# Layer 1's first matrix is applied to a batch's 256 state rows, and the softmax weights multiply the result

## The chip, the cores and the metric

The kernel runs on one core of a Trainium2 chip. The metric is the device time of one execution in microseconds. The names of the engines are those of the profile: PE (TensorE) does matmuls, PEld loads their weights, DVE (VectorE), ACT (ScalarE) and POOL (GpSimd) work on elements, and SP's queue issues the transfers.

## The reference

Three steps follow each other: attention between 512 tokens and 32 states for each of 8 batches and 8 heads (head size 64), a layer normalisation with a two-matrix block and a residual, and a gated convolution block. The 544 tokens of a batch are the 512 token reads and the 32 state reads. All weights are float64.

```python
scores = scale * np.matmul(x, state.transpose(0, 1, 3, 2))
...
xread = np.matmul(a, state)                  # a: softmax over the 32 states
...
sread = np.matmul(a2, x)                     # a2: softmax over the 512 tokens
return np.concatenate([xread, sread], axis=2).astype(np.float32)
...
mu = np.mean(x, axis=-1, keepdims=True)
var = np.mean((x - mu) ** 2, axis=-1, keepdims=True)
xn = (x - mu) / np.sqrt(var + 1e-06) * g_ln
ch = np.maximum(xn @ w_ch1, 0.0) @ w_ch2     # 512 -> 2048 -> 512
return (x + ch).astype(np.float32)
...
h = np.maximum(x @ w_in, 0.0)                # 512 -> 1024
...
return (h * gate @ w_out).astype(np.float32) # gate: sigmoid of a 3-tap convolution of h
```

## The kernel before

Everything is held transposed: features on the 128 partitions, tokens along the free axis. A product in nearly full precision is three matmuls of numbers that are split into a high and a low part (`three`, lines L565 to L567). The float64 words of a weight are taken apart, joined and split by a chain that runs over ACT (L184, L185), DVE (L190, L191), POOL (L192), ACT (L219) and POOL (L220), one slice of 512 KB at a time (class `Converter`).

Layer 1 runs in units: batches 0 to 6, then the tail unit (the 256 state reads of all batches together, `NB`, 256 columns), then batch 7 (`LAST`). In a unit, `L1(u, m)` makes 128 of the 2048 hidden values for all tokens in the bank `ph`, contracting 512 features in four chunks; ACT (L583) and DVE (L584) make the two parts `hH` and `hL` of its relu; and `L2(u, m, n)` adds its contribution to the four banks `acc`. The loop over m from 0 to 15 calls `L1(u, m + 1)` and `L2(u, m)`. Between them it advances a generator, `tasks`, with the attention and the layer normalisation of the next batch, which use the two banks `pat`. At the end of a unit `residual` adds `acc` to the batch's tokens `XT` (L595) and stores them to DRAM (L597). Layer 2 follows after all units.

Attention makes scores twice: tokens by states, and states by tokens (`scores`, L254, in plain fp32, two matmuls that each fill 64 of the bank's 128 partitions). The softmax weights of the tokens, transposed (32 states of four heads fill the 128 partitions), multiply the states to give the token reads: `token_read`, L335 and L336, two matmuls of 512 columns for each 128 features, eight per batch. `lnorm` takes mean and variance by matmuls with a matrix of ones (L487, L488), subtracts the mean (L500), and multiplies by one over the deviation (L510); `xn_split` multiplies by `gcol` and splits into `xnH` and `xnL` (L523, L524), on which L1 works.

Batch 0 has a path of its own through the start (`tokens_start`, in two halves of 256 columns), and while units 0's products run, the weights of layer 1 are still being converted: `need` waits for the slice, and `order` lists in which order the slices are converted. The order of the instructions on each engine is set by the tile scheduler from the program's order, its priorities and its own model of the times.

Of the kernel before, what the change touches and what calls it, by code (L numbers as in the profile page):

```python
# [42 lines left out]
def kernel(  # L43
# [29 lines left out]
    xnH = new("xnH", [KC, S], F32R)  # L73
    xnL = new("xnL", [KC, S], F32R)
# [5 lines left out]
    s_bd = new("s_bd", [KC, 64])  # L80
    s_raw = new("s_raw", [KC, P])
    s_H = new("s_H", [KC, P], F32R)
    s_L = new("s_L", [KC, P], F32R)
    ident = new("ident", [P])
# [10 lines left out]
    spare = [f"w{a}_{m}" for m in range(LATE, M1) for a in (1, 2)]  # L95

    WARM = 8
    START = "s00ws0abab01cac0001b10w1a0cb010a011bL1wcaLbLwc1wLc11L1LwLLLLLL"

    EARLY = 6  # L100
# [15 lines left out]


# [11 lines left out]
    def load_raw(b, s):  # L129
        for hh in range(2):  # L130
            r = 64 * s + 32 * hh
            nc.sync.dma_start(
                s_raw[r : r + 32, :, 64 * hh : 64 * hh + 64],
                state[b].rearrange("(q hh) n d -> hh n q d", hh=2)[hh],
            )
# [33 lines left out]

    def load_rows(tag, w, m):  # L170
# [23 lines left out]
    class Converter:  # L194


        def __init__(self, total, temps, sub):
            self.total, self.temps, self.sub = total, temps, sub
# [14 lines left out]
        def third(self):  # L213
            if self.n2 < self.n1:
                i = self.n2
                (tag, _), t = self.raw[i], self.tmp[i]
                self.done[i] = new(tag, [2, DM], F32R)
# [16 lines left out]
    def prep_state():  # L234
        V.transpose(s_bd.rearrange("p q m -> p (q m)"), s_in.rearrange("p q h r -> p (q h r)"))
        state_parts()

    def state_parts(sub=V):
        A.activation(s_H, s_raw, AF.Copy)
        for ql in range(2):  # L240
            r = slice(64 * ql, 64 * ql + 64)

            def part(t):
                return t[r].rearrange("p (g ql) m -> p ql g m", g=2)[:, ql]

            sub.tensor_tensor(part(s_L), part(s_raw), f32(part(s_H)), op=ALU.subtract)
# [4 lines left out]
    def scores(b, g, xT):  # L251
        sc = bank()
        for ql in range(2):
            T.matmul(  # L254
                sc[64 * ql : 64 * ql + 64, :], s_bd[:, 2 * g + ql, :], xT[:, ql, :],
# [727 lines left out]
```

## Time and profile before

| | us |
|---|---|
| median of 3 runs | 1287.51 (1287.22 to 1288.11) |
| the profiled execution | 1287.5 |
| its span, first to last instruction | 1285.7 |
| busy: PE / DVE / ACT / POOL | 1245.7 / 692.1 / 459.5 / 283.6 |

The span is what the profile's rows add up to; the execution's time is 1.8 us longer. A busy PE is one that had a matmul in flight: its rows overlap, so the cost of one is read from start to start, its pitch, and not from its duration. An "x4" or "x2" in a row of PE counts instructions: an fp32 matmul is two of them.

### The profile page before, as it was taken

The page shows a single profiled execution, that of the slowest core. Times are in us where ns is not written, and L with a number is a line of the kernel's source. Part 1 is how long each engine was busy: PE and PEld are TensorE (multiplying, and loading weights), DVE is VectorE, ACT ScalarE, POOL GpSimd, SP SyncE. Part 2 cuts the span into 40 slices and gives each one's busy share as a digit, 9 for nine tenths or more (in the row PEclk, how much of TensorE's full clock was granted, in tenths as well). Part 3 has the DMA queues.
Part 4 walks back from the last instruction along what each step waited for, and adds up shares of the span by engine and source line. Part 5 has one row for each costly group of instructions (what it writes and reads, how often), then busy time and mean ns, then how long its engine had stood idle before and what let it go on. Part 6 is the DMA issues. An engine that isn't in the chain of part 4 may idle for free.

```text
span 1285.7 us, 15045 instructions
## 1 busy us (share of the span) xinstructions
PE 1245.7 (97%) x5827; PEld 1000.4 (78%) x5827; DVE 692.1 (54%) x1050; ACT 459.5 (36%) x807; POOL 283.6 (22%) x381
## 2 busy tenths in 40 slices
PE   6888899999999999999999999999999999999997
PEld 5665677877787877877877889888888888888885
DVE  5999974444444443444444332544555665566653
ACT  5855432222232222222222222445343343344332
POOL 3477701101101100200200210343233222122210
PEclk9899999999999999999999999999999999999999
DMA  9641022012012002012003000333110111110001
GB/s 310 182 115 52 5 66 39 17 47 42 17 49 40 17 34 52 20 35 48 17 1 82 1 23 28 108 91 107 57 49 23 61 66 32 42 67 1 33 33 41
DMA packets 126148, 69.10 MB, mean 54 GB/s; under 512 B 103268, under 2 KB 115580, under 8 KB 125052
## 3 DMA queue, kind: packets, MB, share of 16 engines
q1 hardware_dynamic: 126076, 68.14, 18.9%
q8 instruction: 45, 0.74, 0.2%
q14 instruction: 27, 0.22, 0.1%
HBM read 50.82 MB, written 17.30 MB: 53 GB/s over the span
## 4 chain that ended last, share of the span: by engine, by line
PE 87%; DVE 7%; DMA 1%; SPq 1%; issue 1%; POOL 1%; ACT 1%; DVEq 0%; POOLq 0%
PE acc L565 14%; PE acc L566 14%; PE acc L567 13%; PE ph L567 12%; PE ph L565 12%; PE ph L566 12%; PE pat L565 2%; PE pat L566 2%; PE pat L567 2%; DVE ctmp L191 2%; PE pat L254 1%; PE pat L281 1%; DVE ctmp L190 1%; DMA w<-in_moe_w_ch_dram 1%; PE pat L335 1%
## 5 line engine op out<-in xcount | busy, mean ns | idle before, releaser
L565 PE MATMUL ph<-xnH,w 128*128 128x512 f32 (+1 forms) x684 | 258.1, 377 | 2.9 <-DVE w L584 1.4
L566 PE MATMUL ph<-xnL,w 128*128 128x512 f32 (+1 forms) x684 | 257.8, 377 | 1.4 <-POOL xnL L467 1.4
L567 PE MATMUL ph<-xnH,w 128*128 128x512 f32 (+1 forms) x684 | 257.5, 376 | 0.2 <-POOL w L220 0.2
L566 PE MATMUL acc<-hL,w 128*128 128x512 f32 (+1 forms) x560 | 213.6, 385 | 6.4 <-DVE hL L584 6.4
L567 PE MATMUL acc<-hH,w 128*128 128x512 f32 (+1 forms) x560 | 212.1, 382 | 0.0
L584 DVE SCALAR_TENSOR_TENSOR hL<-ph,hH 128x512 fp32r<-128x512 f32 (+1 forms) x142 | 92.4, 651 | 198.8 <-ACT hH L583 198.2
L565 PE MATMUL acc<-hH,w 128*128 128x512 f32 (+1 forms) x560 | 188.2, 383 | 0.1
L583 ACT ACTIVATE hH<-ph 128x512 fp32r<-128x512 f32 (+1 forms) x142 | 80.3, 566 | 278.8 <-PE ph L567 267.1
L565 PEld LDWEIGHTS ph<-xnH,w 128*128 128x128 f32 x684 | 128.7, 188 | 34.1 <-issue 5.0
L567 PEld LDWEIGHTS ph<-xnH,w 128*128 128x128 f32 x684 | 129.0, 189 | 30.2 <-issue 5.7
L566 PEld LDWEIGHTS ph<-xnL,w 128*128 128x128 f32 x684 | 128.8, 188 | 27.2 <-POOL xnL L467 1.9
L566 PEld LDWEIGHTS acc<-hL,w 128*128 128x128 f32 x560 | 105.6, 189 | 31.4 <-DVE hL L584 10.5
L900 DVE SCALAR_TENSOR_TENSOR w<-w,cw,w 128x544 f32<-128x544 f32 x128 | 105.3, 823 | 45.8 <-POOL w L898 44.0
L567 PEld LDWEIGHTS acc<-hH,w 128*128 128x128 f32 x560 | 105.7, 189 | 22.1 <-issue 1.0
L565 PEld LDWEIGHTS acc<-hH,w 128*128 128x128 f32 x560 | 101.7, 189 | 22.4 <-issue 0.7
L566 PE MATMUL acc<-w,w 128*128 128x512 f32 x272 | 107.8, 396 | 0.0
L565 PE MATMUL acc<-w,w 128*128 128x512 f32 x272 | 107.3, 395 | 0.0
L567 PE MATMUL acc<-w,w 128*128 128x512 f32 x272 | 105.7, 396 | 0.0
L479 POOL TENSOR_TENSOR bR<-XT 128x512 f32<-128x512 f32 x12 | 16.5, 1376 | 378.3 <-ACT XT L369 377.8
L881 ACT ACTIVATE w<-w 128x544 f32<-128x544 f32 x64 | 42.2, 659 | 150.8 <-DVE w L900 150.7
L882 DVE TENSOR_TENSOR w<-w,w 128x544 f32<-128x544 f32 x64 | 46.7, 729 | 51.9 <-ACT w L881 51.9
L888 DVE TENSOR_TENSOR w<-w,w 128x512 fp32r<-128x512 f32 x64 | 46.8, 731 | 42.6 <-ACT w L887 40.4
(284 smaller groups left out, 1790.6 us busy)
## 6 DMA issues: line engine op xcount, KB each, us to landing
w<-in_moe_w_ch_dram SPq DMA_DIRECT2D x32, 512.0 KB, 6.8
out_dram<-w SPq DMA_DIRECT2D x34, 256.0 KB, 2.2
x2d<-XT SPq DMA_DIRECT2D x8, 1024.0 KB, 3.9
bP<-in_x_dram SPq DMA_DIRECT2D x104, 64.0 KB, 2.5
bP<-in_x_dram SPq DMA_DIRECT2D x24, 256.0 KB, 3.3
bP<-x2d SPq DMA_DIRECT2D x8, 512.0 KB, 3.8
bQ<-x2d SPq DMA_DIRECT2D x8, 512.0 KB, 4.4
w<-in_moe_w_in_dram SPq DMA_DIRECT2D x8, 512.0 KB, 3.7
```

The costliest lines, as they stand in the source:

```text
L190: V.tensor_scalar(t, t, 3, None, op0=ALU.logical_shift_left)
L191: V.scalar_tensor_tensor(t, hi, -(2**31), t, op0=ALU.bitwise_and, op1=ALU.bitwise_or)
L479: add.tensor_tensor(sp, src[:, 0:2], src[:, 2:4], op=ALU.add)
L565: T.matmul(o, lh, rh, start=first, stop=False)
L566: T.matmul(o, lh, rl, start=False, stop=False)
L567: T.matmul(o, ll, rh, start=False, stop=last)
L583: A.activation(h, p, AF.Relu)
L584: V.scalar_tensor_tensor(l, p, 0.0, f32(h), op0=ALU.max, op1=ALU.subtract)
L881: A.activation(c, c, AF.Sigmoid)
L882: V.tensor_tensor(c, c, h[:, 1 : SEQ + 1], op=ALU.mult)
L888: V.tensor_tensor(g[:, 1], c[:, :S], f32(g[:, 0]), op=ALU.subtract)
L900: V.scalar_tensor_tensor(c, h[:, k : k + SEQ], cw[:, k * FF + f : k * FF + f + 1], c, op0=ALU.mult, op1=ALU.add,)
```

## The change

The token reads are a product of the softmax weights A (256 rows: 8 heads x 32 states) with the states, laid out block by block. So L1 of the tokens is the same as A times Z, where Z is (states less their mean) times (g times W1): 256 rows by 2048. L1 then contracts 256 rows and not 512 features, and has six matmuls where it had twelve (L597 to L599). One over the deviation of the layer normalisation is positive and one number per token, so it passes through the relu and the second matrix, and `residual` multiplies by it (L648) before it adds (L650).

Added is the making of Z. Each batch has eight tiles (`z_tile`: 4 column blocks `j` of 512 by 2 halves `g` of the states), each with two fp32 matmuls of 64 partitions (L562) into a bank `pat`, one DVE instruction that subtracts the mean (L569), and the split into `ZH` on ACT (L572) and `ZL` on DVE (L573), through one buffer `zc`. A second `Z` pair lets block j + 1 be made while block j is used. The first matrix is converted in unit 0 only, times g, in rows and unsplit, written to DRAM (`w1d`), and from unit 1 on streamed back in pieces of 512 KB through a ring of seven buffers (`pass_pairs`, L556), eight pieces per batch.

`token_read` contracts only the 64 rows that a group of 128 features needs, and has three matmuls for it where it had two: twelve per batch (L361). L510 and the splits of the normalised tokens (L523, L524) are gone. For the tail unit L1 is a product in plain fp32 (L625), of the streamed pieces and the normalised state reads. Batch 0 no longer makes its normalised tokens in the start; Z of block j is made when four slices of the first matrix are converted (`z_first`), and slices are converted four of the first, four of the second matrix a time.

```diff
-    def token_weights_3(aT, Y):
-
-        A.activation(Y[0:64, 0], aT[0:64], AF.Copy)
-        A.activation(Y[64:128, 1], aT[64:128], AF.Copy)
-        V.tensor_tensor(Y[64:128, 0], aT[0:64], f32(Y[0:64, 0]), op=ALU.subtract)
-        V.tensor_tensor(Y[0:64, 1], aT[64:128], f32(Y[64:128, 1]), op=ALU.subtract)
-
-    def token_read(xr, q, Y):
-        T.matmul(xr, s_H[:, q], Y, start=True, stop=False)
-        T.matmul(xr, s_L[:, q], Y, start=False, stop=True)
...
+    def token_weights_3(aT, b, g, c):
+        h, l = (t[:, g, c] for t in parts[b])
+        A.activation(h, aT, AF.Copy)
+        V.tensor_tensor(l, aT, f32(h), op=ALU.subtract)
+
+    def token_read(b, g):
+
+        h, l = (t[:, g] for t in parts[b])
+        xr = [bank(), bank()]
+        for i, (s, a) in enumerate(((s_H, h), (s_L, h), (s_H, l))):
+            for ql in range(2):
+                r = slice(64 * ql, 64 * ql + 64)
+                T.matmul(xr[ql], s[r, 2 * g + ql], a[r], start=i == 0, stop=i == 2)
+        for ql in range(2):
+            A.activation(XT[b][:, 2 * g + ql], xr[ql], AF.Copy)
...
+    def pass_pairs(n):
+
+        for _ in range(n):
+            i = passed[0]
+            if i == len(stream):
+                return
+            passed[0] += 1
+            _, j, g = stream[i]
+            t = pieces[stream[i]] = new(f"r{i % RING}", [2, S])
+            nc.sync.dma_start(flat(t), w1d[j, g])
+
+    def z_tile(u, j, g, w):
+
+        zp = bank()
+        for ql in range(2):
+            T.matmul(
+                zp[64 * ql : 64 * ql + 64], sbd[u][:, 2 * g + ql], w[:, ql], start=True, stop=True
+            )
+        if g == 0:
+            Z[u, j] = [new(f"Z{c}{j % 2}", [2, S], F32R) for c in "HL"]
+        h, l = (t[:, g] for t in Z[u, j])
+        f = new("zc", [S])
+        V.scalar_tensor_tensor(
+            f, colsum[j // 2][:, j % 2], nbars[u][:, g : g + 1], zp, op0=ALU.mult, op1=ALU.add
+        )
+        A.activation(h, f, AF.Copy)
+        V.tensor_tensor(l, f, f32(h), op=ALU.subtract)
+
+    def z_step(u, j, g):
+        z_tile(u, j, g, pieces[u, j, g])
+        pass_pairs(1)
+
+    def z_first(j):
+
+        for q in range(KC):
+            need(1, KC * j + q)
+        w = rounded[2 * j : 2 * j + 2]
+        sums = new("zc", [S])
+        G.tensor_tensor(sums, w[0][:, 0], w[0][:, 1], op=ALU.add)
+        for q in range(2):
+            G.tensor_tensor(sums, sums, w[1][:, q], op=ALU.add)
+        vp = bank()
+        T.matmul(vp, ones1, sums, start=True, stop=True)
+        A.activation(colsum[j // 2][:, j % 2], vp, AF.Copy)
+        for g in range(2):
+            z_tile(0, j, g, w[g])
+            nc.sync.dma_start(w1d[j, g], flat(w[g]))
...
-        cols_product(p, w1[m], *([t[:, k, c] for k in range(KC)] for t in (xnH, xnL)))
...
+    def L1(u, m):
+        c = slice(P * (m % 4), P * (m % 4) + P)
+        if u < NB:
+            p = ph[m % 2]
+            (wh, wl), (ah, al) = Z[u, m // 4], parts[u]
+            for g in range(2):
+                three(p, wh[:, g, c], wl[:, g, c], ah[:, g], al[:, g], g == 0, g == 1)
+        else:
+            p = ph[m % 2][:, :TAIL]
+            for k in range(KC):
+                w = pieces["t", m // 4, k // 2][:, k % 2]
+                T.matmul(p, w[:, c], tns[NB][:, k], start=k == 0, stop=k == KC - 1)
+            if m % 4 == 3:
+                pass_pairs(2)
+        relu_parts(m, p)
...
-            V.tensor_tensor(dst[:, d, :n], dst[:, d, :n], acc[d][:, :n], op=ALU.add)
...
+        for d in range(KC):
+            V.tensor_tensor(t[d], acc[d], rstd[u], op=ALU.mult)
+        for d in range(KC):
+            V.tensor_tensor(XT[u][:, d], XT[u][:, d], t[d], op=ALU.add)
+        nc.sync.dma_start(x2d[u], flat(XT[u]))
...
+            if u == 0 and m % 4 == 2 and m < 12:
+                z_first(m // 4 + 1)
+            elif m % 4 < 2 and 0 < u < NB and m < 12:
+                z_step(u, m // 4 + 1, m % 4)
+            elif m in (12, 13) and ahead is not None:
+                z_step(ahead, 0, m - 12)
```

The order of the instructions moves in three places that matter below. First PE, in unit 1, at `L1(1, 13)`. Before, its twelve matmuls stand together, four such groups of three (two of them here):

```order
L565 MATMUL ph1_84<-xnH_1_63,w1_13_157_1192 128x512
L566 MATMUL ph1_84<-xnL_2_64,w1_13_157_1192 128x512
L567 MATMUL ph1_84<-xnH_1_63,w1_13_157_1192 128x512
L565 MATMUL ph1_84<-xnH_1_63,w1_13_157_1192 128x512
L566 MATMUL ph1_84<-xnL_2_64,w1_13_157_1192 128x512
L567 MATMUL ph1_84<-xnH_1_63,w1_13_157_1192 128x512
```

After the change, the last tile of block 3 (`r0`, `sbd1`: batch 1) and the first of the next batch (`r1`, `sbd0`) stand at this place, both in the bank `pat1`, then the second halves of `L1` for m = 12 and 13 with the matmuls of the layer normalisation (L467, L468) in between:

```order
L599 MATMUL ph1_83<-AH1_107_647,ZL1_251_1703 128x512
L562 MATMUL pat1_85<-r0_199_1240,sbd1_109_649 64x512 x2
L562 MATMUL pat1_85<-r1_201_1268,sbd0_206_1331 64x512 x2
L597 MATMUL ph0_82<-AH1_107_647,ZH1_250_1702 128x512
L598 MATMUL ph0_82<-AL1_108_648,ZH1_250_1702 128x512
L597 MATMUL ph1_83<-AH1_107_647,ZH1_250_1702 128x512
L598 MATMUL ph1_83<-AL1_108_648,ZH1_250_1702 128x512
L467 MATMUL pat0_84<-bQ_260_1750,ones_11_73 128x512
L599 MATMUL ph0_82<-AH1_107_647,ZL1_251_1703 128x512
L599 MATMUL ph1_83<-AH1_107_647,ZL1_251_1703 128x512
L468 MATMUL pat0_84<-bQ_260_1750,ones_11_73 128x512
L562 MATMUL pat1_85<-r3_215_1393,sbd0_206_1331 64x512 x2
```

What moved: an L1 is in two halves of three matmuls here, and the second half stands right behind the tile of Z that it reads.

Second PE, in unit 1, at the token read of batch 2. Before, two matmuls for each bank:

```order
L566 MATMUL ph0_83<-xnL_2_64,w1_2_58_334 128x512
L567 MATMUL ph0_83<-xnH_1_63,w1_2_58_334 128x512
L335 MATMUL pat0_85<-bQ_185_1601,s_H_9_71 128x512
L336 MATMUL pat0_85<-bQ_185_1601,s_L_10_72 128x512
L565 MATMUL acc0_79<-hH_3_65,w2_1_95_728 128x512
L335 MATMUL pat1_86<-bQ_185_1601,s_H_9_71 128x512
L336 MATMUL pat1_86<-bQ_185_1601,s_L_10_72 128x512
```

After, three for each, and those of the second bank stand twenty rows further on:

```order
L298 MATMUL pat1_85<-bP_213_1362,bV_221_1419 64x128 x8
L361 MATMUL pat0_84<-AH0_204_1329,s_H_6_68 128x512
L361 MATMUL pat0_84<-AH0_204_1329,s_L_7_69 128x512
L361 MATMUL pat0_84<-AL0_205_1330,s_H_6_68 128x512
L597 MATMUL acc0_78<-hH_1_63,w2_3_68_417 128x512
L598 MATMUL acc0_78<-hL_2_64,w2_3_68_417 128x512
L599 MATMUL acc0_78<-hH_1_63,w2_3_68_417 128x512
```

The rows of one bank stand together, so matmuls of the two row halves do not alternate here (they do in some other batches).

Third DVE, at the end of unit 1. Before, four additions from the banks `acc`, and then the relu of the next unit:

```order
L595 TENSOR_TENSOR XT1_91_706<-XT1_91_706,acc0_79 128x512
L324 TENSOR_TENSOR bU_218_2155<-bU_218_2155,m10_219_2156 128x512
L595 TENSOR_TENSOR XT1_91_706<-XT1_91_706,acc1_80 128x512
L595 TENSOR_TENSOR XT1_91_706<-XT1_91_706,acc2_81 128x512
L325 STREAM_TRANSPOSE bR_221_2181<-bU_218_2155 128x512
L595 TENSOR_TENSOR XT1_91_706<-XT1_91_706,acc3_82 128x512
L584 SCALAR_TENSOR_TENSOR hL_4_66<-ph0_83,hH_3_65 128x512
L331 TENSOR_TENSOR bQ_223_2216<-bR_221_2181,bQ_223_2216 64x512
```

After, four multiplications from the banks, and the relu parts (L612) of the next unit between the additions:

```order
L648 TENSOR_TENSOR tn_267_1891<-acc0_78,rs1_165_1058 128x512
L648 TENSOR_TENSOR tn_267_1891<-acc1_79,rs1_165_1058 128x512
L333 TENSOR_REDUCE m10_285_1991<-bU_284_1990 128x16
L310 RECIPROCAL z20_283_1986<-z20_283_1986 128x1
L648 TENSOR_TENSOR tn_267_1891<-acc2_80,rs1_165_1058 128x512
L648 TENSOR_TENSOR tn_267_1891<-acc3_81,rs1_165_1058 128x512
L650 TENSOR_TENSOR XT1_106_646<-XT1_106_646,tn_267_1891 128x512 x2
L612 SCALAR_TENSOR_TENSOR hL_2_64<-ph0_82,hH_1_63 128x512
L334 TENSOR_TENSOR bU_284_1990<-bU_284_1990,m10_285_1991 128x512
L311 TENSOR_SCALAR rm0_289_2047<-hmask_14_76,z20_283_1986 128x2
L650 TENSOR_TENSOR XT1_106_646<-XT1_106_646,tn_267_1891 128x512
L612 SCALAR_TENSOR_TENSOR hL_2_64<-ph1_83,hH_1_63 128x512
```

The relu of the next unit's first L1 now has six instructions of the residual ahead of it, where it had four.

## Rows read from the trace of the kernel before

**Rows 1.** The page: the span, and the busy time of the engines.

```profile
span 1285.7 us, 15045 instructions
...
PE 1245.7 (97%) x5827; PEld 1000.4 (78%) x5827; DVE 692.1 (54%) x1050; ACT 459.5 (36%) x807; POOL 283.6 (22%) x381
```

**Rows 2.** Windows: length, then each engine's busy time, granted clock, DMA share, GB/s.

```profile
80.00:100.00 20.00, 18.08 (x86) 13.78 (x85) 19.77 (x25) 11.52 (x21) 15.23 (x11) 0.91 0.22 65
140.00:160.00 20.00, 17.21 (x70) 12.42 (x69) 19.03 (x23) 8.54 (x13) 13.70 (x10) 1.00 0.02 4
160.00:180.00 20.00, 20.00 (x82) 14.48 (x82) 15.32 (x26) 7.69 (x13) 0.00 (x0) 1.00 0.12 26
267.80:366.00 98.20, 98.20 (x445) 76.20 (x445) 47.48 (x85) 27.26 (x46) 8.45 (x8) 1.00 0.15 35
814.00:901.00 87.00, 87.00 (x383) 70.98 (x382) 40.94 (x66) 41.31 (x71) 34.65 (x32) 1.00 0.38 116
```

**Rows 3.** Timeline of PE, steady stretch: start, us, line, operation, tiles.

```profile
300.50 0.39 PE L565 MATMUL ph<-xnH,w 128*128 128x512 f32 x1
300.73 0.39 PE L566 MATMUL ph<-xnL,w 128*128 128x512 f32 x1
```

**Rows 4.** Timeline of PE in the tail unit, matmuls of 256 columns.

```profile
769.01 0.28 PE L566 MATMUL ph<-xnL,w 128*128 128x256 f32 x1
769.13 0.28 PE L567 MATMUL ph<-xnH,w 128*128 128x256 f32 x1
```

**Rows 5.** Timeline of PE, unit 2, both halves of a score product together.

```profile
295.39 0.40 PE L566 MATMUL ph<-xnL,w 128*128 128x512 f32 x1
295.71 1.08 PE L254 MATMUL pat<-bQ,s_bd 128*64 128x512 f32 x4
296.72 0.50 PE L567 MATMUL ph<-xnH,w 128*128 128x512 f32 x1
297.06 0.39 PE L565 MATMUL ph<-xnH,w 128*128 128x512 f32 x1
```

**Rows 6.** Timeline of PE, unit 1, one half of a score product alone.

```profile
267.76 1.07 PE L254 MATMUL pat<-bQ,s_bd 128*64 128x512 f32 x2
268.76 0.50 PE L567 MATMUL ph<-xnH,w 128*128 128x512 f32 x1
```

**Rows 7.** Timeline of PE, unit 2, where the token read begins.

```profile
310.09 0.51 PE L335 MATMUL pat<-bQ,s_H 128*128 128x512 f32 x1
310.44 0.39 PE L336 MATMUL pat<-bQ,s_L 128*128 128x512 f32 x1
```

**Rows 8.** Timeline of PE in the start, four fp32 matmuls of 256 columns.

```profile
27.55 1.99 PE L457 MATMUL pat<-w,w 128*128 128x256 f32 x8
29.20 0.58 PE L694 MATMUL acc<-hL 128*128 128x512 f32 x1
```

**Rows 9.** Groups of instructions, 267 to 660 us: busy us, mean ns, idle before.

```profile
L584 DVE SCALAR_TENSOR_TENSOR hL<-ph,hH 128x512 fp32r<-128x512 f32 x64 | 44.1, 689 | 103.2 <-ACT hH L583 102.7
L583 ACT ACTIVATE hH<-ph 128x512 fp32r<-128x512 f32 x64 | 38.3, 598 | 156.4 <-PE ph L567 144.8 <-DVE tn L510 10.0 <-DVE bQ L485 1.5
...
L595 DVE TENSOR_TENSOR XT<-XT,acc 128x512 f32<-128x512 f32 x16 | 10.2, 679 | 1.3 <-PE acc L567 1.3
...
L517 DVE SCALAR_TENSOR_TENSOR bV<-pat,eps,bV 128x512 f32<-128x512 f32 x4 | 3.0, 746 | 0.1
```

**Rows 10.** Timeline of DVE at the first residual of units 0 and 6.

```profile
179.66 0.69 DVE L595 TENSOR_TENSOR XT<-XT,acc 128x512 f32<-128x512 f32 x1 [0.64 <-PE acc L567]
...
766.41 1.29 DVE L595 TENSOR_TENSOR XT<-XT,acc 128x512 f32<-128x512 f32 x2 [1.27 <-PE acc L567]
```

**Rows 11.** The page: DMA issues, KB each, median us from issue to landing.

```profile
w<-in_moe_w_ch_dram SPq DMA_DIRECT2D x32, 512.0 KB, 6.8
...
bP<-x2d SPq DMA_DIRECT2D x8, 512.0 KB, 3.8
```

**Rows 12.** Waits of SP's queue: us in total, times, longest.

```profile
SPq L597 <- DVE XT L595: 206.3, 7, 39.6
```

More of the change, by code (lines that the diff above doesn't have):

```diff
@@ L216, in third @@
                 (tag, _), t = self.raw[i], self.tmp[i]
+                g = self.gain(i)
+                if g is not None:
+                    self.done[i] = g[0]
+                    A.activation(g[0].rearrange("p (k c) -> p k c", c=P), t, AF.Copy, scale=g[1])
+                    self.n2 += 1
+                    return
                 self.done[i] = new(tag, [2, DM], F32R)
@@ L620, in need @@
         conv_a.ensure(min(i + AHEAD, conv_a.total - 1))
-        (w1 if a == 1 else w2)[m] = conv_a.done[i]
+        return conv_a.done[i]
     def temp(i):
@@ L649 @@
     xnt[0, 0], xnt[0, 1] = (x0.rearrange("p ck h d -> p h ck d")[:, 4 * g : 4 * g + 4] for g in range(2))
[L650 removed]
+    for i, (a, m) in enumerate(order):
+        if m < (RAWS if a == 1 else LATE):
+            load_weight(i)
     load_xt(1, 0, new("bP", [1024]))
[L652 removed]
+    cbuf = sb.tile([24, 2 * DM], I32, tag=spare[0], name="cbuf")
     craw, c0 = cbuf[:, 0:256], f32(cbuf[:, 256:384]).rearrange("p (k c) -> p k c", c=P)
     nc.sync.dma_start(craw, i32(conv_w).rearrange("k (f c) -> (k f) c", f=FF))
[L656 removed]
     G.memset(eps, EPS_LN)
[L658 to L661 removed]
+    ones1 = new("ones1", [P])
+    G.memset(ones1, 1.0)
+    A.activation(ones, ones1, AF.Copy, scale=1.0 / DM)
     for q in range(4):
@@ L723, in states_start @@
     def states_start():
-        starts = [work, {"V": spare[6], "R": spare[7], "s": "1"}]
+        starts = [work, {"V": spare[5], "R": spare[6], "s": "1"}]
         E2Ts, z2s = [], []
@@ L798 @@
         n = S if u < NB else TAIL
-        nxt = S if follow != NB else TAIL
         if u == NB:
@@ L805 @@
             tasks = chain(attend(LAST), tail_norm())
+        elif u == 0:
+            tasks = chain(token_norm(0), next_tokens(1))
         else:
             tasks = next_tokens(follow)
+        ahead = LAST if follow == NB else follow if u < NB and u != LAST else None
         if u == 0:
+            for g in range(2):
+                token_read(0, g)
             for _ in states_start():
                 pass
+            z_first(0)
+            L1(0, 0)
         for m in range(M1):
-            if m < M1 - 1 and not (u == 0 and m + 1 < EARLY):
-                if u == 0:
-                    need(1, m + 1)
-                L1(u, m + 1, slice(0, n))
+            if m < M1 - 1:
+                L1(u, m + 1)
+            if u == 0 and m == 3:
+                for k in range(LATE, M1):
+                    load_weight(place_of[2, k])
+            if u == 0 and m == M1 - 4:
+                pass_pairs(RING)
             if u == LAST:
-                load_b(m)
                 if m == 2:
```

309 lines of the change are left out of this document (135 added, 174 removed).

## Prediction

> **What bounds the kernel now.** I read the engines' busy times first: PE is busy 1245.7 of 1285.7 us, no other engine over 54% [rows 1]. Then the windows, to see where the rest lies. In a unit of layer 1 (267.8 to 366 us) PE is busy in all 98.2 us at full granted clock, DVE for 47.5, ACT 27.3, POOL 8.5, and transfers take 15% of the queues' engines; the stretch before the last unit's end (814 to 901) reads alike [rows 2]. Until about 160 us it is DVE that is full (19.8 of 20, 19.0 of 20), since it converts the weights, while PE has gaps [rows 2]. So layer 1 from 180 us on is a sum of matmuls: whatever leaves PE shortens it, and whatever is put on PE, or makes PE wait, lengthens it. Before 160 us matmuls cost nothing and DVE's work does.
>
> The unit of account is a matmul's pitch, not its duration: 300.73 less 300.50 is 0.23 us for 512 columns though each row says 0.39 [rows 3]; over longer stretches it is 0.229. For 256 columns it is 0.117 to 0.12 [rows 4]. A whole unit takes (766.41 - 179.66) / 6 = 97.8 us from residual to residual [rows 10].
>
> **L1.** Six matmuls go at each of 16 m: 96 x 0.229 = 22.0 us per batch. Units 1 to 6 and the last batch have nothing but PE in their way: 7 x 22.0 = 154 us. Unit 0 is dealt with below.
>
> **Z.** No row is a tile of Z, but the score product has the same form: fp32, two matmuls of 64 weight columns and 512 data columns. Its four instructions stand between the starts 295.39 and 297.06, with one ordinary matmul on each side of them: 1.67 - 2 x 0.23 = 1.21 us for the pair [rows 5]. Half of it alone takes from 267.76 to 268.76, as long as both do from 295.71 to 296.72 [rows 6]: the two column halves run side by side if they are adjacent, and cost twice if something stands between. In the order of the changed kernel nearly all pairs are adjacent. Units 1 to 6 have 8 each and the tail unit has 6 (for the last batch): 54 x 1.21 = 65.3 us, and three broken pairs add 3 x 1.2 = 3.6. Sum +69.
>
> The Trainium skill, "TensorEngine Tiling (Array Packing)", Key Properties, says that a change of the tiling mode drains the engine; that speaks against a change that sets 54 pairs and a token read of another shape among full-width matmuls. The Trainium skill, "FP8 and Floating Point Precision", TensorE Precision Notes, counts four passes for true fp32, by which a pair would be 4 x 0.229 = 0.92 us, or +50 for 54, without the drain. The pair's 1.21 holds both, so the trace agrees, and the sum goes by it.
>
> **The token read.** Twelve matmuls where eight were: 4 x 0.229 = 0.92 us per batch. A contraction over 64 rows isn't in the trace. The first ordinary matmul after another form is followed after 0.35 and not 0.23 us [rows 7], so I count 0.12 for a change of form: in and out of four groups of three, 1.0 us. Six batches: 12 us. From below, if matmuls of the two row halves ran side by side, as column halves do, twelve would cost six pitches, 0.5 us less than before; from above, a change at each of the twelve, 2.4 us more. Since one bank's rows mostly stand together I take the middle price, and keep -3 to +14.
>
> **Tail unit.** Twelve matmuls of 256 columns (1.41 us) become four in fp32. Four such took 27.55 to 29.20 = 1.65 us [rows 8]; with 0.12 for the change of form 1.77. Sixteen times 0.36 is +5.8 us.
>
> **What DVE, ACT and POOL gain and lose** beside PE. DVE gets per batch 8 x (0.75 + 0.69) for Z (L517 and L584 are such instructions [rows 9]) and 4 x 0.68 more in the residual, and loses L510 and the splits: about +6 on 47 us while a unit shrinks from 98 to some 87. ACT gains 8 x 0.6. That is 55 and 30 of 87 us; averages don't bind. The residual does two things in a row: four multiplications set `acc` free in 4 x 0.68 = 2.7 us, and PE has two L1s (2.75 us) to do before it writes there. It is just covered, so I cost it at nothing; uncovered it would be under 1 us per unit.
>
> **The stream.** From unit 1 on eight pieces of 512 KB per 87 us, some 48 GB/s more, go out while 15% of the transfer engines' time is used [rows 2]. A piece lands after 4 to 7 us [rows 11]. It is asked for when its buffer's last reader is done, five to seven pieces (over 50 us) ahead. But SP works in order, and waits up to 39.6 us for residuals before it can store [rows 12]. Pieces queued behind that store are the third and later ones of the next unit, so a lead remains. Nothing added; in the tail unit the order leaves about 40 matmuls (8 us) between a request and its reader, and 0 to 5 us may be lost there.
>
> **Waits for Z.** A tile goes through PE (1.0), DVE (0.75), ACT (0.6), DVE (0.69) [rows 5, 9]: 3.0 us and the handing over. It is hidden where PE has other rows in between. In the order it has, except at the last block of units 1, 3 and 5, where two tiles follow each other in the same bank: the second must wait until DVE has read the first, and then the halves of L1 until ZL is there. DVE's queue also holds the normalisation then. Nothing of the kind is in the trace; from below 0, from above the chain once more at each of two blocks, 6 us per unit. I take 2 us, six times: +12.
>
> **Unit 0 and the start.** They are bound by DVE [rows 2]. The change takes the first half-batch normalisation out and puts in that of the whole batch, 8 tiles and an L1 that can't begin before four slices are converted. Giving each DVE instruction of the two orders its duration from rows like those of DVE [rows 9], up to unit 0's residual I come to 115 us before and 116 after, and before the last conversion to 94 and 91. POOL has 12 additions in place of 16 subtractions. What PE has left after the last block's Z is ready is some 20 us, as before (157 to 180 us). So 0, from -10 (PE's shorter L1s count) to +20 (each Z of block j comes late, since PE then has nothing but L2s to fill in).
>
> **The sum**: -154 + 69 + 12 + 6 + 12 + 0 = -55 us. On the profiled execution's 1287.5 us, equal to the median, that gives 1232.
>
> **The rivals.** *No waits at all.* PE is full from 180 us on, the row halves overlap, unit 0 gains a little: 1232 - 12 - 15 - 5 = 1200. For it speaks that DVE has 30 us to spare in a unit; against it that a full window of PE was reached with buffers in pairs, while all tiles of Z share one `zc` and two banks with attention. Chance of 1200 to 1220: 0.18.
>
> *The start grows.* Blocks of unit 0 come one after the other: conversion of four slices, sums on POOL, Z, L1, and the first relu some 25 us later than before. If PE then lags at each of the four blocks by 5 to 8 us beyond the above, +20 to +30: 1250 to 1262. For it speaks that DVE is at 99% in that stretch [rows 2], so that any late Z has no slack to catch up in; against it that PE has gaps in the same stretch. 0.17.
>
> *Z waits at every block.* This is the one on the other side. There are four blocks a unit, 24 in six units, and 67 us are gained without waits for Z (55 + 12). If the chain of 3.0 us is exposed at each, because attention holds the bank or DVE is at something else, 24 x 3.0 = 72 us are lost: 1292, slower. It decides at 67 / 24 = 2.8 us a block; at 2 us the result is 1268. A second price would come on top: where PE was busy 18.1 of 20 us, its granted clock fell to 0.91 [rows 2]. Against it: in the order, L2's twelve matmuls (2.7 us) stand between most tiles and their first reader. Chance of ending above 1266: 0.14.
>
> A tile whose two halves run one after the other is a smaller rival: 54 x 1.2 = +65, about 1297. The two score rows speak against it; 0.02, counted with the one before.
>
> **How the numbers follow.** The forecast (1220 to 1250) has 0.49, the others as given: without waits 0.18, longer start 0.17, waits throughout 0.16 with the broken pairs. 1232 is the likeliest; 1200 to 1266 leaves out 2 in 10. A measurement of this kernel can tell about 0.2%, 2.6 us, from no change. Of the 0.16, half ends beyond that on the slow side, a quarter within it: faster 0.88, same 0.04, slower 0.08.
>
> **What would show it.** Right: ph matmuls drop by half; a unit from residual to residual takes 86 to 90 us; a tile of Z shows two starts 1.2 us apart around it; waits of PE in units appear only at block 3 and stay under 5 us per unit; unit 0's residual begins between 170 and 200 us; layer 2 is as long as before. Wrong: a unit over 92 us with idle PE before L597 or L562, released by DVE; a row of the tile at 1.6 us or more; unit 0's residual after 205 us; SP waiting for a store while PE waits for a piece.

## The result, and the profile after

| | before | after |
|---|---|---|
| median, us | 1287.37 (1286.22 to 1288.11, 4 runs) | 1240.82 (1240.1 to 1240.98, 4 runs) |
| profiled execution / its span | 1287.5 / 1285.7 | 1240.1 / 1238.3 |

The ratio is 0.9638, with a 95% interval of 0.9621 to 0.9655: 3.6% faster. 1232 was forecast, 1200 to 1266 as the range, so the time lies inside, 9 us above the forecast value. By stretches (below) two errors are larger than that and of opposite sign, so the nearness of the number is in part luck.

The page of the changed kernel: the span, the busy times, the granted clock in 40 slices, and the pieces of the stream (KB each, us to landing).

```profile
span 1238.3 us, 14035 instructions
...
PE 1166.8 (94%) x5179; PEld 859.3 (69%) x5179; DVE 752.3 (61%) x1142; ACT 462.3 (37%) x808; POOL 277.9 (22%) x370
...
PEclk7587899999999999999999999999999999999999
...
r<-w1d SPq DMA_DIRECT2D x64, 512.0 KB, 3.4
```

Against [rows 1], PE's busy time falls by 79 us and the span by 47: PE now has 72 us without work, where it had 40, and its clock's row of digits begins with 7, 5, 8, 7. That is the start; the page of the kernel before has there:

```profile
PEclk9899999999999999999999999999999999999999
```

The rest of the reading goes by where the units end. The timeline of DVE has the first multiplication of each residual (L648):

```profile
193.63 0.69 DVE L648 TENSOR_TENSOR tn<-acc,rs 128x512 f32<-128x512 f32 x1 [0.83 <-PE acc L599]
...
285.44 0.68 DVE L648 TENSOR_TENSOR tn<-acc,rs 128x512 f32<-128x512 f32 x1
...
372.81 0.68 DVE L648 TENSOR_TENSOR tn<-acc,rs 128x512 f32<-128x512 f32 x1
...
720.19 0.69 DVE L648 TENSOR_TENSOR tn<-acc,rs 128x512 f32<-128x512 f32 x1 [0.72 <-PE acc L599]
...
855.94 0.68 DVE L648 TENSOR_TENSOR hL<-acc,rs 128x512 f32<-128x512 f32 x1
```

These answer to [rows 10]. Unit 0 ends at 193.6 and not at 179.7. Units 1 to 6 take 720.19 - 193.63 = 526.6 us where they took 586.8. What comes after, the tail unit, batch 7 and layer 2, takes 1238.3 - 720.2 = 518.1 us where it took 1285.7 - 766.4 = 519.3. The sum of the three is the change of the span:

| stretch | forecast | measured |
|---|---|---|
| start and unit 0 | 0 (-10 to +20) | +14.0 |
| units 1 to 6 | -49 | -60.2 |
| tail unit, batch 7, layer 2 | -6.5 | -1.2 |
| span | -55 | -47.4 |

The forecasts by stretch are those of the prediction, summed as its terms fall: six batches' L1, 48 tiles, one broken pair, the token reads and the waits in the middle row; one batch's L1, six tiles, two broken pairs and the fp32 L1 in the last.

**The steady units.** Windows of units 1 and 2 (length, then PE, PEld, DVE, ACT and POOL busy, clock, transfers):

```profile
193.60:285.40 91.80, 90.34 (x395) 61.27 (x395) 53.48 (x92) 27.91 (x48) 8.41 (x8) 1.00 0.31 86
285.40:372.80 87.40, 87.40 (x388) 60.00 (x387) 49.92 (x88) 27.30 (x46) 8.46 (x8) 1.00 0.32 86
```

Unit 2 is 87.4 us long, with PE busy all through and DVE for 50 us of it; units 3 to 5 are as long within 0.1 us. This answers the window of one unit in [rows 2]. Unit 1 has 4.4 us more: a score product more than the others (1.2), a torn tile (1.2), and 1.5 us without work on PE. Waits of PE in all six units are few (engine and line, what it waited for, total, times, longest):

```profile
PE pat L562 <- DVE zc L569: 2.5, 3, 0.9
PE acc L598 <- DVE hL L612: 0.6, 1, 0.6
```

Those are 3.1 us where 12 were forecast. A tile of Z looks as the score product did. The timeline of PE at the last block of unit 3, the place that the prediction named:

```profile
439.37 1.08 PE L562 MATMUL pat<-r,sbd 128*64 128x512 f32 x4 [0.85 <-DVE zc L569]
440.38 0.50 PE L597 MATMUL ph<-AH,ZH 128*128 128x512 f32 x1
440.71 0.39 PE L598 MATMUL ph<-AL,ZH 128*128 128x512 f32 x1
...
442.43 1.08 PE L562 MATMUL pat<-r,sbd 128*64 128x512 f32 x4
443.44 1.20 PE L597 MATMUL acc<-hH,w 128*128 128x512 f32 x4
```

The first tile there waited 0.85 us for DVE, which had the bank; it holds PE from 439.37 to 440.38, and the matmul after it is followed after 0.33, not 0.23 us. That is [rows 5] again.

**The start.** Up to the end of unit 0 the windows of the changed kernel and of the one before are, in this order:

```profile
0.00:160.00 160.00, 106.22 (x423) 68.49 (x424) 129.72 (x175) 90.71 (x159) 91.17 (x80) 0.75 0.57 173
160.00:193.60 33.60, 31.18 (x128) 19.65 (x127) 21.15 (x34) 11.93 (x19) 0.00 (x0) 1.00 0.30 86
```

```profile
0.00:160.00 160.00, 129.14 (x630) 98.81 (x631) 137.98 (x196) 96.51 (x181) 100.19 (x91) 0.94 0.47 133
160.00:179.60 19.60, 19.60 (x79) 14.17 (x79) 14.98 (x25) 7.69 (x13) 0.00 (x0) 1.00 0.12 27
```

DVE worked 150.9 us after and 153.0 before: the sum of its work did not change, as forecast. But it was done with it 14 us later, since it stood idle for 43 us in place of 27. All of the difference lies behind 60 us: from there to the residual it is idle for 26.4 us in place of 8.5. Its longest waits there:

```profile
DVE zc L569 <- PE pat L562: 7.7, 3, 3.5
DVE hL L612 <- ACT hH L611: 7.7, 4, 3.5
```

It waits for PE's tile, and for ACT's relu, which waits for PE. And PE waits for DVE in turn. The timeline of PE at the start of block 1, with idle time and its releaser in brackets:

```profile
98.38 0.74 PE L599 MATMUL ph<-AH,ZL 128*128 128x512 f32 x2
102.37 1.08 PE L271 MATMUL pat<-bQ,sbd 128*64 128x512 f32 x4 [3.24 <-DVE bQ L368]
103.68 0.53 PE L597 MATMUL ph<-AH,ZH 128*128 128x512 f32 x1 [0.24 <-ACT ZH L572]
104.02 0.62 PE L598 MATMUL ph<-AL,ZH 128*128 128x512 f32 x1
104.44 0.63 PE L597 MATMUL ph<-AH,ZH 128*128 128x512 f32 x1
104.86 0.63 PE L598 MATMUL ph<-AL,ZH 128*128 128x512 f32 x1
106.03 1.22 PE L599 MATMUL ph<-AH,ZL 128*128 128x512 f32 x2 [0.54 <-DVE ZL L573]
```

PE waits 3.24 us for a transposition on DVE that the next batch's scores need, then for ZH, ZL and the relu. The pitch of two neighbours (104.44 to 104.86) is 0.42 us where it was 0.23 before the waits: the granted clock is 0.50, its lower level (1.2 GHz), from 104 us on for some 13 us, after six us in which PE was busy for 2.5.

The profile's chain, from the last instruction back to what released each step, shows the turns too. Shares by line from 60 us to unit 0's residual, before and after:

```profile
by line: DVE ctmp L191 14.2%; DVE ctmp L190 9.5%; issue 6.4%; DVE XTt L190 5.4%; DVE XTt L191 5.0%; PE acc L565 3.7%; POOL ctmp L192 3.3%; POOL w L220 3.1%; PE acc L566 2.8%; DVE hL L584 2.6%; PE acc L567 2.5%; PE ph L565 2.5%; DVE s_L L246
```

```profile
by line: PE acc L598 9.0%; PE acc L599 8.4%; DVE ctmp L197 7.1%; issue 6.5%; PE acc L597 5.8%; DVE ctmp L198 4.6%; PE pat L562 3.9%; DVE tn L480 3.5%; DVE XTt L198 3.4%; DVE zc L569 3.2%; DVE ZL L573 3.2%; DVE XTt L197 3.2%; PE ph L599 2.8%
```

Summed by engine, DVE has 77.5 us of the chain before and PE 22.7, nearly all of it behind 158 us. After, DVE has 56.9 and PE 52.5. PE's share includes 149.9 to 166.8 us, where it works through L1 and L2 of one block without a wait before it comes to Z of the next.

### The profile page after: what moved, and what is told of

Its sections match the earlier page's. It is cut to its first block, busy times and chain, and to the rows that moved or that the text cites. A ratio compares the mean times of both kernels' runs of the same rounds, so it can differ in the third digit from the quotient of the medians.

```text
span 1238.3 us, 14035 instructions
## 1 busy us (share of the span) xinstructions
PE 1166.8 (94%) x5179; PEld 859.3 (69%) x5179; DVE 752.3 (61%) x1142; ACT 462.3 (37%) x808; POOL 277.9 (22%) x370
## 4 chain that ended last, share of the span: by engine, by line
PE 85%; DVE 7%; DMA 3%; SPq 2%; issue 1%; ACT 1%; POOL 0%; DVEq 0%; POOLq 0%; ACTq 0%
PE acc L598 15%; PE acc L599 14%; PE acc L597 14%; PE ph L597 8%; PE ph L599 8%; PE ph L598 8%; PE pat L562 5%; PE ph L625 2%; PE pat L597 2%; PE pat L598 2%; PE pat L599 2%; PE pat L361 2%; PE pat L298 1%; DVE ctmp L197 1%; SPq L150 1%
## 5 line engine op out<-in xcount | busy, mean ns | idle before, releaser
L598 PE MATMUL acc<-hL,w 128*128 128x512 f32 (+1 forms) x576 | 223.8, 391 | 8.6 <-DVE hL L612 8.5
L599 PE MATMUL acc<-hH,w 128*128 128x512 f32 (+1 forms) x576 | 221.4, 387 | 0.0
L597 PE MATMUL acc<-hH,w 128*128 128x512 f32 (+1 forms) x576 | 174.4, 396 | 2.7 <-ACT hH L611 2.7
L612 DVE SCALAR_TENSOR_TENSOR hL<-ph,hH 128x512 fp32r<-128x512 f32 (+1 forms) x144 | 93.4, 653 | 103.4 <-ACT hH L611 103.2
L597 PEld LDWEIGHTS acc<-hH,w 128*128 128x128 f32 x576 | 104.7, 190 | 48.3 <-ACT hH L611 20.0
L599 PEld LDWEIGHTS acc<-hH,w 128*128 128x128 f32 x576 | 110.0, 191 | 24.7 <-issue 3.6
L597 PE MATMUL ph<-AH,ZH 128*128 128x512 f32 x256 | 105.0, 411 | 3.9 <-ACT ZH L572 3.9
L599 PE MATMUL ph<-AH,ZL 128*128 128x512 f32 x256 | 102.4, 409 | 3.4 <-DVE ZL L573 2.8
L598 PE MATMUL ph<-AL,ZH 128*128 128x512 f32 x256 | 103.2, 404 | 0.0
L569 DVE SCALAR_TENSOR_TENSOR zc<-v,nbar,pat 128x512 f32<-128x512 f32 x64 | 47.5, 743 | 53.6 <-PE pat L562 53.4
L562 PE MATMUL pat<-r,sbd 128*64 128x512 f32 x256 | 72.6, 617 | 4.7 <-DVE zc L569 3.1
L597 PEld LDWEIGHTS ph<-AH,ZH 128*128 128x128 f32 x256 | 48.9, 191 | 28.1 <-ACT ZH L572 10.3
L572 ACT ACTIVATE ZH<-zc 128x512 fp32r<-128x512 f32 x64 | 40.2, 629 | 64.8 <-DVE zc L569 64.8
L599 PEld LDWEIGHTS ph<-AH,ZL 128*128 128x128 f32 x256 | 48.4, 192 | 21.9 <-DVE ZL L573 6.7
L970 POOL TENSOR_SCALAR w<-w,cw 128x544 f32<-128x544 f32 x64 | 47.9, 748 | 62.1 <-ACT w L966 58.7
```

Source lines behind the costliest of these rows:

```text
L562: T.matmul(zp[64 * ql : 64 * ql + 64], sbd[u][:, 2 * g + ql], w[:, ql], start=True, stop=True)
L569: V.scalar_tensor_tensor(f, colsum[j // 2][:, j % 2], nbars[u][:, g : g + 1], zp, op0=ALU.mult, op1=ALU.add)
L597: T.matmul(o, lh, rh, start=first, stop=False)
L598: T.matmul(o, lh, rl, start=False, stop=False)
L599: T.matmul(o, ll, rh, start=False, stop=last)
L612: V.scalar_tensor_tensor(l, p, 0.0, f32(h), op0=ALU.max, op1=ALU.subtract)
```

## The experiments

Each is the changed kernel with one edit, unless it says otherwise. Unit ends are from the profile, times are medians.

**A tile of Z twice.**

```diff
-        for ql in range(2):
+        for ql in 2 * [0, 1] if u else [0, 1]:
             T.matmul(
                 zp[64 * ql : 64 * ql + 64], sbd[u][:, 2 * g + ql], w[:, ql], start=True, stop=True
```

> Every tile of Z from batch 1 on has its two matmuls issued twice (the second time into the same bank), 54 of them where PE is full. If a tile costs PE 1.21 us and nothing hides it: 1240.8 + 65 = 1306 us; if only the way in and out of the other form costs and the passes themselves are cheap, under +25; if PE waits for the chain of Z behind the tile anyway, so that matmuls there are free: under +10.

Measured: 1286.7 us (one run), +46 for 56 more pairs (three of them stand in unit 0), 0.82 us each. That lies between the first two expectations. PE's timeline there shows a doubled tile:

```profile
418.06 1.94 PE L562 MATMUL pat<-r,sbd 128*64 128x512 f32 x8
419.93 0.50 PE L599 MATMUL ph<-AH,ZL 128*128 128x512 f32 x1
```

Eight instructions take 1.87 us where four took 1.01. So a pair is 0.86 us of passes, and 0.35 us of the 1.21 is the way into the other form and back, paid once. The total gives a little less, since the added passes also fill waits: units 1 to 6 have 0.4 us of them here in place of 3.1.

**L1 with twelve matmuls again.**

```diff
-            for g in range(2):
-                three(p, wh[:, g, c], wl[:, g, c], ah[:, g], al[:, g], g == 0, g == 1)
+            halves = [0, 0, 1, 1] if u else [0, 1]
+            for i, g in enumerate(halves):
+                three(p, wh[:, g, c], wl[:, g, c], ah[:, g], al[:, g], i == 0, i == len(halves) - 1)
```

> L1 of batches 1 to 7 has each of its six matmuls twice, twelve again (the sums in it count double). If the forecast's first term is right: 7 x 22.0 = +154, 1395 us. If part of L1's place was already filled with waits for Z (the rival with waits at every block), the added matmuls cover them: +80 to +140.

Measured: 1398.5 us (one run), +157.7, or 22.5 us per batch. The first term of the forecast holds, and the rival that has waits under L1 falls: all that the added matmuls could fill were the 3.1 us of waits in units 1 to 6 and 3.0 us behind them. The mean is not a clean price, though. Units 1 to 6 grow by 23.6 us each and all that follows by 17.6 in sum, and the order differs: in units 2 to 5 a score product has its halves apart here.

**No stream.** The first seven pieces are loaded, and later tiles read them again.

```diff
             _, j, g = stream[i]
+            if i >= RING:
+                pieces[stream[i]] = pieces[stream[i - RING]]
+                continue
```

> The stream of the first matrix stops after the first seven pieces: later tiles of Z read a piece that is already there (so Z is of the wrong block). If the stream is hidden: 1240.8 within 2 us. If pieces come late behind the stores in SP's queue or the transfers slow something down: 5 us or more shorter, and the tail unit above all.

Measured: 1234.1 us, ratio 0.9595 (0.9579 to 0.9611), against 0.9638 with the stream. Units 1 to 6 keep their length to 0.1 us (194.24 to 720.79): there 48 more GB/s (86 in place of 38 in unit 2) cost nothing. From the end of unit 6 on it is 6.5 us shorter, 511.6 us, near the 512.8 that the forecast makes of that stretch. In the changed kernel the order tears two of the last batch's tiles in halves; the two halves of one, in PE's timeline of the tail unit:

```profile
751.67 1.07 PE L562 MATMUL pat<-r,sbd 128*64 128x512 f32 x2
...
758.68 1.07 PE L562 MATMUL pat<-r,sbd 128*64 128x512 f32 x2
```

Without the stream they are adjacent, here two tiles in a row:

```profile
756.14 1.94 PE L565 MATMUL pat<-r,sbd 128*64 128x512 f32 x8
```

Two torn tiles cost some 2 us more, and the 3.0 us that PE waits for ACT and DVE in that stretch are gone too; 1 to 2 us are left without a cause. By its time the second expectation came in, for this stretch only. Its reason isn't shown: in the changed kernel PE waits for no piece there, and what differs in the rows is the order. Other kernels below keep the stream and are some 3 us shorter in the same stretch.

**Batch 0's normalisation left out.**

```diff
-            tasks = chain(token_norm(0), next_tokens(1))
+            rstd[0] = new("rs0", [S])
+            G.memset(rstd[0], 1.0)
+            tasks = next_tokens(1)
```

> The layer normalisation of batch 0 is left out (one over the deviation is set to 1). Unit 0 ends 14 us later than before. If the normalisation, which came into unit 0 from the start, is what holds it up (DVE's 10 us of it stand ahead of the first blocks): 6 to 10 us shorter. If the conversion of the weights sets the pace, or the waits at the start of each block: 0 to 3 us shorter.

Measured: 1227.7 us, ratio 0.9548 (0.9533 to 0.9563): 13 us shorter, more than either expectation had. Unit 0 ends at 191.2, only 2.5 earlier, but unit 1 at 276.3 in place of 285.4. The next batch's attention stands behind the normalisation in the list of tasks and is further on without it: in its unit 1 PE has 376 matmuls where the changed kernel has 395, a score product and a tile of Z fewer among them, and no waits in place of 1.5 us. About 3 us more come in the last units, where this kernel has 0.4 us of waits in place of 3.0. Other edits of the start show the same 3 us there, so it belongs to the order that the scheduler happens to find, not to the normalisation.

**The same normalisation after batch 1's attention.**

```diff
-            tasks = chain(token_norm(0), next_tokens(1))
+            tasks = chain(attend(1), token_norm(0), token_norm(1))
```

> The layer normalisation of batch 0 comes after batch 1's attention in the list of tasks, and not ahead of it; its result is needed only by the residual of unit 0. Leaving it out gave 13 us. If its place ahead of the attention is what costs (the attention is pushed back, into unit 1): 6 to 12 us shorter than 1240.8. If DVE's work on it costs wherever it stands: 0 to 3 us.

Measured: 1235.0 us, 0.9590 (0.9573 to 0.9607), 5.8 us shorter, at the edge of the first expectation. Unit 0 ends at 189.7, 3.9 us earlier, with the same work of DVE by then (151.7 us, 150.9 in the changed kernel); 1.5 us of the rest come behind unit 6. So its place costs something, but most of what leaving it out gave is not to be had by moving it.

**Its partial sums on POOL.**

```diff
-        yield from lnorm(XT[u], new("tn", [KC, S]), S, work, V if u < 2 else G, rstd[u])
+        yield from lnorm(XT[u], new("tn", [KC, S]), S, work, G, rstd[u])
```

> The partial sums of that normalisation (and of batch 1's) go from DVE to POOL, 8 additions each. If DVE's load in the start holds unit 0 up: 2 to 5 us shorter than 1240.8. If the waits at the start of each block do, or POOL becomes late with its part of the conversion: no change to 5 us longer.

Measured: 1234.6 us, 0.9592 (0.9574 to 0.9610). By the time alone, 6.2 us shorter, the first expectation would come nearest. By the profile it doesn't hold: unit 0 ends at 192.5, 1.1 us earlier, unit 1 at 284.3, also 1.1, and the rest is the 3 us in the last units.

**Half of DVE's conversion left out.**

```diff
-        V.scalar_tensor_tensor(t, hi, -(2**31), t, op0=ALU.bitwise_and, op1=ALU.bitwise_or)
+        if t.shape[0] < P or late[0]:
+            V.scalar_tensor_tensor(t, hi, -(2**31), t, op0=ALU.bitwise_and, op1=ALU.bitwise_or)
```

> In the conversion of layer 1's weights the second of DVE's two instructions is left out (the signs and low bits are wrong): 32 x 0.65 to 1.4 us of DVE before 160 us. If DVE's total work sets the end of unit 0, as the forecast had it: 15 us or more shorter than 1240.8. If the chain at the start of each block and the low clock do: 0 to 6 us.

Measured: 1226.6 us, 0.9518 (0.9497 to 0.9539), 14 us shorter, which by itself can't be told from the first expectation's 15. The residual of unit 0:

```profile
182.32 0.68 DVE L651 TENSOR_TENSOR tn<-acc,rs 128x512 f32<-128x512 f32 x1
```

Unit 0 ends 11.3 us earlier. Up to that residual DVE has 32 instructions fewer and 121.7 us of work in place of 150.9, and it is idle for 61 us in place of 43. So 29 us of DVE's work bring 11, less than half. The expectations took one or the other for the whole, and by the profile both miss.

**PE kept at work.** `fill` adds zeros to a bank, 18 matmuls in each of blocks 1 to 3.

```diff
             if u == 0 and m % 4 == 2 and m < 12:
                 z_first(m // 4 + 1)
+                fill(12)
...
+            if u == 0 and m in (4, 8, 12):
+                fill(6)
```

> In unit 0, 18 matmuls that add zeros to one of the banks of acc stand at the start of blocks 1 to 3, where PE waits (54 matmuls, 12 us at full clock). If PE's falling to 1.2 GHz behind those waits costs the 8 us that the pitches there show (0.426 for 0.229 us in some 40 matmuls): 3 to 8 us shorter than 1240.8. If DVE and the chains set the pace and a slow PE only eats its own waits: no change to 8 us longer.

Measured: 1250.6 us, 0.9713 (0.9694 to 0.9732), 9.7 us longer. Unit 0 ends at 206.9, 13 us later, about the 12 us that the added matmuls take at full clock. They did not all lie in the waits, and PE still waits for DVE:

```profile
PE acc L598 <- DVE hL L612: 11.1, 3, 5.6
```

Nor did they keep the clock up: from 60 us to unit 0's residual it is 0.89 in the mean in place of 0.87, and the stretch at the lower level only moved (0.54 from 112 to 122 us). So this run doesn't show what the lower clock costs. It does show that matmuls in the start are not free here: 12 us of them cost 13.

**The column sums on PE.** In the changed kernel POOL adds up four slices for each block. Its timeline shows the last block's three additions (L585, L587) among its parts of the conversion (L199, L233), though the last slice that they need was there at 139.9 us:

```profile
144.41 1.49 POOL L585 TENSOR_TENSOR zc<-r 128x512 f32<-128x512 f32 x1
145.85 1.73 POOL L233 TENSOR_TENSOR w<-ctmp,w 128x512 fp32r<-128x512 f32 x1
...
149.22 1.28 POOL L199 TENSOR_TENSOR ctmp<-ctmp,w 128x512 int32<-128x512 int32 x1
150.46 1.29 POOL L587 TENSOR_TENSOR zc<-zc,r 128x512 f32<-128x512 f32 x1
...
155.85 1.30 POOL L587 TENSOR_TENSOR zc<-zc,r 128x512 f32<-128x512 f32 x1
```

```diff
-        sums = new("zc", [S])
-        G.tensor_tensor(sums, w[0][:, 0], w[0][:, 1], op=ALU.add)
-        for q in range(2):
-            G.tensor_tensor(sums, sums, w[1][:, q], op=ALU.add)
         vp = bank()
-        T.matmul(vp, ones1, sums, start=True, stop=True)
+        for q in range(KC):
+            T.matmul(vp, ones1, w[q // 2][:, q % 2], start=q == 0, stop=q == KC - 1)
```

> The column sums of the first matrix times g, which each block of Z needs, are made by PE alone (four fp32 matmuls with a matrix of ones, added up in the bank) and not by three additions on POOL and one matmul. In the changed kernel the three additions for the last block stand among POOL's part of the conversion of the second matrix, from 144 to 157 us, though the last slice of the first matrix was ready at 140. If that place holds back Z of each block, and with it unit 0: 4 to 9 us shorter than 1240.8, less 4 us for twelve more fp32 matmuls where PE is full. If DVE's pace alone sets it: no change to 4 us longer.

Measured: 1234.9 us, 0.9602 (0.9588 to 0.9617). Unit 0 ends at 190.7, 2.9 us earlier, and the other 3 us are again in the last units. At unit 0's end that lies within the first expectation, but its reason is not borne out. In the changed kernel PE comes to its matmul of the sums (L589) at 89.2, 131.6 and 166.6 us in blocks 1 to 3, which is 3.5, 12.4 and 9.5 us after POOL's last addition has ended. It doesn't wait for it; PE's rows at the third:

```profile
166.27 0.39 PE L599 MATMUL acc<-hH,w 128*128 128x512 f32 x1
166.50 0.27 PE L323 MATMUL pat<-ident,bV 128*128 128x128 f32 x1
166.61 1.02 PE L589 MATMUL pat<-zc,ones 128*128 128x512 f32 x2
```

What the trace shows instead is a faster DVE. Up to unit 0's residual its conversion (L197, L198, 32 instructions each) takes 52.9 us in place of 62.1. The length of L197 goes with what POOL does: in the changed kernel's start it is 1.27 us in the mean of the 15 that have POOL at work for over 80% of their time, and 0.42 in all 8 that have it for under 20%. With the sums gone POOL has 75 us of work in the start in place of 91. The edit also takes the sums out of the buffer zc that the tiles use; the run doesn't tell the two apart.

**Three edits together:** the sums on PE, the later normalisation, and POOL for its sums.

> Three edits at once: the column sums on PE, batch 0's normalisation after batch 1's attention, its partial sums on POOL. If the places of these three in the start are separate costs: 8 to 14 us shorter than 1240.8, 1227 to 1233. If they are the same wait seen three times: about what the best of them gives, 1234.

Measured: 1230.2 us, 0.9561 (0.9545 to 0.9577). Unit 0 ends at 188.5, 5.2 earlier, where the three had 2.9, 3.9 and 1.1 alone: partly the same cost.

**A second buffer zc besides.**

```diff
-        f = new("zc", [S])
+        f = new(f"zc{g}", [S])
```

> As the run before, with two buffers zc (one for each half of the states) in place of one. If tiles of Z wait for one another there, as the rival with waits at every block has it: 2 to 6 us shorter than the run before. The steady units show 3 us of waits in all, so by the trace no more than 3 there, and the rest only in unit 0.

Measured: 1231.2 us, 0.9572 (0.9558 to 0.9586): the same time as the run before. But unit 0 ends at 181.5, 7.0 earlier; units 1 to 6 then take 531.4 us in place of 526.6, and what follows 2.0 us more. The tiles did wait for each other in the one buffer, in unit 0. Later there was nothing to win, and in the order that the scheduler found PE waits for 6.9 us in units 1 to 6 in place of 3.1.

**The second buffer in unit 0 only.**

```diff
-        f = new("zc", [S])
+        f = new(f"zc{0 if u else g}", [S])
```

> As the run with three edits, with the second buffer zc used in unit 0 alone. With it in all units unit 0 ended 7 us earlier, and units 1 to 6 and the last batch were 7 us longer together. If the two effects are apart (unit 0's tiles wait for one another in one buffer; the steady units lose by another order of instructions): 1223 to 1225 us. If the order after unit 0 hangs on unit 0's own end: 1229 to 1232 again.

Measured: 1226.8 us, 0.9533 (0.9520 to 0.9546), 1.1% under the change as it was made, between the two expectations and nearer the first. The residuals of units 0 and 1:

```profile
182.01 0.69 DVE L645 TENSOR_TENSOR tn<-acc,rs 128x512 f32<-128x512 f32 x1 [0.58 <-PE acc L596]
...
276.16 0.68 DVE L645 TENSOR_TENSOR tn<-acc,rs 128x512 f32<-128x512 f32 x1
```

Unit 0 ends at 182.0, 11.6 us earlier than in the changed kernel, but unit 1 takes 94.2 us, 2.4 more, so a part comes back. Two thirds of what the start had lost is found. The second buffer's part of it is a matter of the chain alone: with one buffer and with two DVE has the same work up to unit 0's residual, 132.9 and 133.0 us, and the residual comes 6.4 us earlier.

## Why the prediction was right, and where its steps failed

**L1: right.** -22.0 us per batch was forecast, and 22.5 is what putting the matmuls back costs in the mean. PE is the bound from unit 1 on, before and after.

**Z: right.** 1.21 us per tile shows in the rows, and doubling splits it into 0.86 and 0.35. The Trainium skill's "TensorEngine Tiling (Array Packing)", Key Properties, says that a change of the tiling mode drains the engine; the trace agrees that the change has a price, 0.35 us here. The Trainium skill's "FP8 and Floating Point Precision", TensorE Precision Notes, has four passes for true fp32: the 0.86 us of a repetition is 3.7 of the pitches of [rows 3], so the trace nearly agrees. Tiles that the order had torn in halves are torn in the trace.

**Waits for Z in the steady units: too high.** 12 us were taken, 3.1 measured. The step took the order's two adjacent tiles in one bank for a stall at each, with the chain of 3.0 us half exposed. In the trace the first tile waits under 1 us and the halves of L1 lie between.

**Token read: between its bounds.** The timeline shows a group whose matmuls of one bank stand together, three of them:

```profile
500.70 0.50 PE L361 MATMUL pat<-AH,s_H 64*128 64x512 f32 x1
501.04 0.39 PE L361 MATMUL pat<-AH,s_L 64*128 64x512 f32 x1
501.27 0.39 PE L361 MATMUL pat<-AL,s_H 64*128 64x512 f32 x1
501.60 0.50 PE L597 MATMUL ph<-AH,ZH 128*128 128x512 f32 x1
```

and, in unit 0, one in which the two banks alternate, six of them:

```profile
162.06 0.50 PE L361 MATMUL pat<-AH,s_H 64*128 64x512 f32 x2
162.40 0.39 PE L361 MATMUL pat<-AH,s_L 64*128 64x512 f32 x2
162.63 0.40 PE L361 MATMUL pat<-AL,s_H 64*128 64x512 f32 x2
162.96 0.50 PE L599 MATMUL acc<-hH,w 128*128 128x512 f32 x1
```

Both take 0.90 us. So row halves do run side by side when they alternate, as the lower bound had it. The middle price counted 0.93 us for a group (three pitches and 0.24 us for the change of form) and fits groups like the first: 0.90 from start to next start, and 0.1 more behind it. Most groups are of that kind, but not all.

**What the sum of the steady units lacked.** Units 1 to 6 came out 11.5 us shorter than forecast. Waits are 9 of them. Another 2 come from a term that the prediction did not have: before, one score product in each of units 1, 3 and 5 has its halves apart, which costs 1.0 us more ([rows 6] is one of them), and in the changed kernel none has, though one score product more falls into unit 1. So L1, Z and the token reads together came within 1 us of their sum. Beside PE, the prediction's 55 and 30 us for DVE and ACT are not what its own terms add up to (53 and 32); the window of unit 2 has 49.9 and 27.3, so that neither binds held.

**Unit 0 and the start: the failed step.** "They are bound by DVE", and since DVE's work up to unit 0's residual came out the same, the term was 0. Measured are 14.0 us. The work is the same (153.0 and 150.9 us; the prediction's 115 and 116 were too low, but their difference held). But the old start gave DVE conversions to do whatever PE did, and the new one makes PE and DVE take turns four times: four slices, their sums, two tiles through one buffer, then L1, whose relu needs DVE again. With that PE came into the chain, for 52.5 us of it in place of 22.7, and "Before 160 us matmuls cost nothing" no longer held: 12 us of added matmuls cost 13. Taking 29 us off DVE shortened the start by 11; giving tiles two buffers, in addition to three shifts of work, by 6.4, with DVE's work unchanged; the three shifts by 5.2. So it is a chain with several links, as the rival "the start grows" described, and at a price of 14 us it fell between the forecast and that rival's 20 to 30. The prediction had the mechanism as a rival and its end inside the bounds; it failed to see that an equal sum of work says nothing once the work is in a chain.

**Tail unit: too low.** -6.5 us was forecast for what follows unit 6, and -1.2 measured. PE's busy time falls there by 4.2 us, from 510.2 to 506.0, and it waits for ACT and DVE for 3.0, for which the sum had no term; 2 us more are without a cause. The stream's "0 to 5 us may be lost there" was costed at nothing. Without the stream 6.5 us come back, but in another order, and no row shows PE waiting for a piece. The tail unit's own rows cost what was forecast: PE's fp32 L1 has 1.54 us from its start to the next and 0.2 more behind it, 1.73 against 1.77.

**Clock.** The prediction named 0.91 as a second price of waits. In the start it was worse: 0.75 in the mean of the first 160 us, where it was 0.94. No run had the higher clock alone, so its price stays open. An estimate from the rows: two stretches at the lower level stand on the chain, 112.6 to 117.5 and 149.9 to 155.2 us, 23 matmuls in 10.2 us, which at 0.23 us each would take 5.3. By that the clock could be 5 of the 14 us.

## What to carry to other kernels

A kernel whose one engine is full for most of its span can be costed by pitches, form by form: here that gave the large terms to 3%, and doubling a suspected operation is a cheap proof of its price, if the price is read from the rows: the doubled kernel's total also holds filled waits and another order. Where no engine is full, as in a start, compare the chain and not the sums: see which engines the profile's chain runs through, count how many times two engines hand over to each other for one block, and which single buffer makes the next block wait. And a difference of 3 us between two variants may lie 500 us away from the edit, in another order that a scheduler found; look at where the units end before giving it a cause.

## What the runs showed of the hardware that was not expected

Two matmuls that contract 64 rows each, in different row halves and different banks, run side by side when they are adjacent (six in 0.90 us), and one behind the other when those of one bank come first (three in 0.90 us). An fp32 pair of column halves costs 0.86 us per repetition and 0.35 us once for the change of form. DVE's 128x512 shift of the conversion (L197) takes 0.42 us while POOL rests, and 1.27 us in the mean while POOL works.
